# Decode attention with its MLP on one core: the place of wo's loads, the order at the last V quads, and a V quad in two pieces

## The chip, the cores and the metric

The kernel runs on one core of a Trainium2 chip. The metric is the device time of one execution in microseconds (us); of several executions the median is given. A profiled execution has a trace, from which all finer times here are taken: TensorE (PE) multiplies, and PEld is its weight load; VectorE is DVE, ScalarE is ACT, GpSimd is POOL, SyncE is SP. "SPq" is the time that an instruction which issues a DMA spends in SP's queue.

## The reference

One decode step for 8 batch rows (`B`), one token each, model width 512 (`D`). All is bfloat16 at the interfaces.

```python
x   = A_x                                        # [8, 1, 512]
q   = (layernorm(x) @ wq)                        # 32 heads of 128
k,v = k_cache[:, :, 8192-2048:, :], v_cache[...] # last 2048 positions, 8 kv heads, 4 query heads on each
p   = softmax(q k^T / sqrt(128))
h   = x + (p v as [8, 4096]) @ wo                # wo: [4096, 512], 4 MB
u   = layernorm(h)
# The second part's token shifts are zero for one token, so its first two matmuls add nothing:
x1  = u
out = h + x1 + gelu(layernorm(x1) @ w3) @ w4     # w3: [512, 1792], w4: [1792, 512]
```

The window is 2048 positions, so K and V are 4 MB for each row, 64 MB in all. With wq and wo (4 MB each) and w3 and w4 (1.8 MB each) the core reads 79.2 MB.

## The kernel before, in words

**Loads.** K and V of a row come in two quads each, (row, 0) and (row, 1), of 2 MB: four kv heads with 2048 positions. A quad is one DMA with 128 rows of 16 KB, and lands in one of the `NS` = 8 slots of the tile `ring`. The list `loads` (L240 to L247) is written out by hand; SP issues it in this order, on one hardware queue (L435 to L452): wq, then for each row b its two K quads and the two V quads of row b-2 (`LAG` = 2). After K of row 7 come V (5,0), (5,1), (6,0), (6,1), then wo in four parts of 1 MB (128 x 8 rows of 1 KB each), then V (7,0) and (7,1), and behind the list w3 and w4 (w4 in two parts). `place` numbers the quads in this order; quad n goes to slot n modulo 8 and waits for `taken` of quad n-8, the TensorE operation that read the slot last. wo shares the tile `wbig` with wq and waits only for the q projection, which is over near 17 us. w3 and w4 use the slots of K (7,0) and K (7,1). The last V quad, `LASTV`, is issued as four DMAs of 512 KB with a semaphore each (`sem_l`); `landed` says which semaphore a piece waits for.

**Compute.** Each quad has four pieces (`cq`), so that there are 64 items for K and as many for V. A written-out loop over p orders the instructions of every engine. In step p TensorE transposes item p of K (`pe_T`, 16 matmuls against a permutation, L275), ScalarE and VectorE copy the halves to SBUF (`evict`), TensorE multiplies item p-24 of V (`pe_PV`, 16 matmuls, L365; `LPV` = 24) and item p-2 of K with q (`pe_QK`, L295). The steps of a row's softmax (`softmax_1` to `softmax_5`, L304 to L355) lie between; within a step they stand ahead of `pe_PV`, and `pe_QK` behind it. K's items end at p = 63, so V of row 5 is multiplied at p = 64 to 71, row 6 at 72 to 79 and row 7 at 80 to 87. The last two `pe_QK` of row 7 stand in TensorE's queue behind the first V items of row 5. Each engine runs its own instructions in order.

**The end.** `scale` (L374, VectorE) turns the sums of a quad into `oT_all`. `pe_wo(0)` multiplies heads 0 to 15 with wo (64 matmuls, L388, after four that add x, L384), `pe_wo(1)` heads 16 to 31. In the kernel before, `scale` of quad (7,0) follows its last piece, then comes piece 0 of (7,1), then `pe_wo(0)`, then pieces 1 to 3 of (7,1), the second `scale` and `pe_wo(1)`. Behind that run the layernorm (L471 to L499), w3 (56 matmuls, L490), gelu (L515), w4 (56 matmuls, L527), the transpose and the store.

Of the kernel before, what the change touches and what calls it, by code (L numbers as in the profile page):

```python
# [14 lines left out]
DH = 128  # L15
# [11 lines left out]
NS = 8  # L27
# [6 lines left out]
LAG = 2  # L34
# [32 lines left out]
def bass_sequential_preLN__sliding_block_cached__mixer_s_mlp__decode_kernel(  # L67
# [23 lines left out]
    with es:  # L91
        sb = lambda shape, dtype, name: es.enter_context(nc.sbuf_tensor(name, shape, dtype))
        ps_t = lambda shape, dtype, name: es.enter_context(nc.psum_tensor(name, shape, dtype))
        S = lambda name: es.enter_context(nc.semaphore(name))
# [25 lines left out]
        ring = sb([128, NS, NCQ * DH], dt.bfloat16, "ring")  # L120
# [46 lines left out]
        oT_ps = ps_t([128, 512], dt.float32, "oT_ps")  # L167

        sem_r = [S(f"sem_r{i}") for i in range(NS)]
        sem_l = [S(f"sem_l{i}") for i in range(4)]  # L170
        sem_x, sem_wq, sem_wo, sem_w3, sem_w4a, sem_w4b, sem_out = (
            S(n) for n in ("sem_x", "sem_wq", "sem_wo", "sem_w3", "sem_w4a", "sem_w4b", "sem_out"))
        PE, AC, DV, PO, SP = (Engine(S(n)) for n in ("s_pe", "s_act", "s_dve", "s_pool", "s_sp"))

        def dma(eng, dst, src, sem, *waits):
            def f(e):
                e.dma_start(dst, src).then_inc(sem, 16)
            eng.op(f, *waits, inc=False)
# [62 lines left out]
        for b in range(NB + LAG):  # L241
            if b < NB:
                loads += [("k", b, 0), ("k", b, 1)]
            if b == NB + LAG - 1:
                loads += [("wo", n, 0) for n in range(4)]
            if b >= LAG:
                loads += [("v", b - LAG, 0), ("v", b - LAG, 1)]  # L247
        quads = [l for l in loads if l[0] != "wo"]
        place = {l: n for n, l in enumerate(quads)}
        LASTV = ("v", NB - 1, 1)  # L250
        taken = {}

        def landed(l, cq):
            n = place[l]
            if l == LASTV:
                return sem_l[cq], 16
            return sem_r[n % NS], 16 * (n // NS + 1)

        e_Tlo, e_Thi, e_lo, e_hi, e_QK, e_PV = {}, {}, {}, {}, {}, {}
# [2 lines left out]
        LAST = NB - 1  # L262

        def split(i):
            return i // 8, (i // 4) % 2, i % 4

        def pe_T(i):
            b, j, cq = split(i)
            s = place["k", b, j] % NS

            def half(lo):
                def f(e):
                    for c in range(lo, lo + 8):
                        n = 16 * cq + c
                        ins = e.matmul(kT_ps[i % 2][:, c * 128:(c + 1) * 128],  # L275
                                       ring[:, s, n * DH:(n + 1) * DH], ident_p[:, :], is_transpose=True)
                    return ins
                return f
            e_Tlo[i] = PE.op(half(0), landed(("k", b, j), cq), e_lo.get(i - 2), e_idp)
            e_Thi[i] = PE.op(half(8), e_hi.get(i - 2))  # L280
            taken["k", b, j] = e_Thi[i]

        def evict(i):
            e_lo[i] = AC.op(lambda e: e.activation(kT_sb[:, i % NKT, 0:1024], kT_ps[i % 2][:, 0:1024], ACT.Copy),  # L284
                            e_Tlo[i], e_QK.get(i - NKT))
            e_hi[i] = DV.op(lambda e: e.tensor_copy(kT_sb[:, i % NKT, 1024:2048], kT_ps[i % 2][:, 1024:2048]),  # L286
                            e_Thi[i], e_QK.get(i - NKT))
# [15 lines left out]
        def softmax_1(b):  # L303
            e_max[b] = DV.op(lambda e: e.tensor_reduce(mcol[:, :], S_ps[b % 2][:, :], AX.X, ALU.max),  # L304
                             e_QK[8 * b + 7], e_mT.get(b - 1))

        def softmax_2(b):
            e_mT[b] = PE.op(lambda e: e.matmul(sm[0:1, MROW], mcol[:, :], ident_f[:, :], start=True, stop=True),  # L308
                            e_max[b], e_rL.get(b - 1), e_idf)
            e = DV.op(lambda e: e.tensor_reduce(Mrow[:, :].rearrange("o (h x) -> o h x", h=4),  # L310
                                                sm[0:1, MROW].rearrange("o (h c x) -> o h x c", h=4, c=4),
                                                AX.X, ALU.max), e_mT[b])
            m_bc = bass.AP(tensor=Mrow[:, :].tensor, offset=0, ap=[[H, 1], [8, 4], [0, 4], [1, 8]])
            e_neg[b] = DV.op(lambda e: e.tensor_scalar(negrow[:, :].rearrange("o (h c x) -> o h c x", h=4, c=4), m_bc,
                                                       -1.0, None, ALU.mult), e, e_negps.get(b - 1))

        def softmax_3(b):
            e_negps[b] = PE.op(lambda e: e.matmul(sm[:, NEG], negrow[0:1, :], ones_f[0:1, 0:1],  # L318
                                                  start=True, stop=True), e_neg[b], e_ones)
            j = b % 2  # L320
            e_negc[b] = DV.op(lambda e: e.tensor_copy(negcol[:, j:j + 1], sm[:, NEG]), e_negps[b], e_exp.get(b - 2))  # L321
            e_exp[b] = AC.op(lambda e: e.activation(P_sb[:, :], S_ps[j][:, :], ACT.Exp, bias=negcol[:, j:j + 1],  # L322
                                                    scale=1.0, accum_out=lcol[:, j:j + 1]),
                             e_negc[b], e_sp.get((b - 1, 3)), e_lsel.get(b - 2))
            for r in range(4):
                a, m = P_sb[:, 128 * r:128 * (r + 1)], mask_b[:, :]
                pb = bass.AP(tensor=a.tensor, offset=a.offset, ap=[a.ap[0], [1, 128], [0, 4]])
                mb = bass.AP(tensor=m.tensor, offset=m.offset, ap=[m.ap[0], [0, 128], [1, 4]])
                eng = DV if b == LAST else PO
                e_sp[b, r] = eng.op(lambda e, r=r, pb=pb, mb=mb: e.tensor_tensor(  # L330
                    P4_sb[:, 128 * r:128 * (r + 1), :], pb, mb, ALU.mult),
                    e_exp[b], e_PT.get((b - 1, 3)), e_mask)
# [60 lines left out]
        for p in range(NG + LPV):  # L393
            if p < NG:
                pe_T(p)
                evict(p)
            for b in range(NB):
                base = 8 * b + 7 + LQK
                if p == base + 1:
                    softmax_2(b)  # L400
                elif p == base + 2:
                    softmax_3(b)
                elif base + 4 <= p <= base + 6:
                    softmax_4(b, p - base - 4)
                elif p == base + 7:
                    softmax_5(b)
            i = p - LPV
            if 0 <= i < NG:
                b, j, cq = split(i)
                if (b, j) == (LAST, 1):  # L410
                    dst = kbank[1][:, 0:16]
                    pe_PV(i, dst, e_lo[NG - 1], e_hi[NG - 1], e_lo[NG - 2], e_hi[NG - 2])
                else:
                    dst = oT_ps[:, 16 * j:16 * (j + 1)]
                    pe_PV(i, dst, e_scale.get((b - 1, 1)))
                if (b, j) == (LAST, 0) and cq == 3:
                    scale(b, 0, dst, e_PV[i])
                elif (b, j) == (LAST, 1) and cq == 0:
                    pe_wo(0)
                elif b < LAST and j == 1 and cq == 3:  # L420
                    scale(b, 0, oT_ps[:, 0:16], e_PV[i])
                    scale(b, 1, oT_ps[:, 16:32])
                elif (b, j) == (LAST, 1) and cq == 3:
                    scale(b, 1, dst, e_PV[i])
                    pe_wo(1)
            if 0 <= p - LQK < NG:
                pe_QK(p - LQK)
                b, j, cq = split(p - LQK)
                if (j, cq) == (1, 3):
                    softmax_1(b)  # L430
            if p >= 7 + LQK + 6 and (p - 7 - LQK - 6) % 8 == 0 and (p - 7 - LQK - 6) // 8 < NB:
                softmax_4((p - 7 - LQK - 6) // 8, 3)
# [3 lines left out]
        for l in loads:  # L436
            what, b, j = l
            if what == "wo":
                n, hh = b, H // 4
                dma(SP, wo_v[:, n * hh:(n + 1) * hh, :],  # L440
                    A_wo[n * hh * DH:(n + 1) * hh * DH, :].rearrange("(h p) n -> p h n", p=DH), sem_wo, e_q)
                continue
            n = place[l]
            src = (A_k_cache if what == "k" else A_v_cache)[b, 4 * j:4 * (j + 1), W0:SK, :].rearrange(
                "h (p c) d -> p h (c d)", p=32)
            free = taken[quads[n - NS]] if n >= NS else None
            if l == LASTV:
                for cq in range(4):
                    cs = slice(16 * cq * DH, 16 * (cq + 1) * DH)
                    dma(SP, ring[:, n % NS, cs], src[:, :, cs], sem_l[cq], free)  # L450
            else:
                dma(SP, ring[:, n % NS, :], src, sem_r[n % NS], free)  # L452

# [57 lines left out]
        for n in range(2):  # L511
            cs = slice(n * FH * B, (n + 1) * FH * B)
# [64 lines left out]
```

## Time and profile before

| what | value |
|---|---|
| median of 3 runs | 200.34 us (199.55, 200.34, 200.67) |
| profiled execution | 200.1 us |
| its span | 198.3 us |
| mean granted TensorE clock | 0.853 |
| HBM read | 79.18 MB, 399 GB/s over the span |
| TensorE matmul busy | 151.0 us (76%), 2861 matmuls and 2861 weight loads |
| VectorE, ScalarE, GpSimd busy | 82.5 us, 79.1 us, 32.2 us |
| K quads: 16 of 2 MB | 27.4 us from issue to landing (median) |
| V quads: 15 of 2 MB | 20.4 us |
| V pieces: 4 of 512 KB | 12.2 us |
| wo: 4 of 1 MB | 29.4 us |
| w3; w4 in two parts | 16.8 us; 19.6 and 16.5 us |

The span runs from the first to the last recorded instruction; the 1.8 us between it and the execution's time lie around it. "From issue to landing" holds the time in which a DMA stands behind others in the queue, so it is a measure of the backlog. In rows of the chain and of the timeline the first number is the start and the second the length, both in us. A line of DMA counters such as "q8 instruction: 22, 0.36, 0.6%" gives a queue's packets, MB and share of the 16 DMA engines' time. In the rows of the windows, each engine's busy time and count stand in the order PE, PEld, DVE, ACT, POOL, then the granted clock, the DMA engines' share and GB/s.

### The profile page before, as it was taken

The page shows a single profiled execution, that of the slowest core. Times are in us where ns is not written, and L with a number is a line of the kernel's source. Part 1 is how long each engine was busy: PE and PEld are TensorE (multiplying, and loading weights), DVE is VectorE, ACT ScalarE, POOL GpSimd, SP SyncE. Part 2 cuts the span into 40 slices and gives each one's busy share as a digit, 9 for nine tenths or more (in the row PEclk, how much of TensorE's full clock was granted, in tenths as well). Part 3 has the DMA queues.
Part 4 walks back from the last instruction along what each step waited for, and adds up shares of the span by engine and source line. Part 5 has one row for each costly group of instructions (what it writes and reads, how often), then busy time and mean ns, then how long its engine had stood idle before and what let it go on. Part 6 is the DMA issues. An engine that isn't in the chain of part 4 may idle for free.

```text
span 198.3 us, 6194 instructions
## 1 busy us (share of the span) xinstructions
PE 151.0 (76%) x2861; PEld 125.3 (63%) x2861; DVE 82.5 (42%) x198; ACT 79.1 (40%) x91; POOL 32.2 (16%) x38
## 2 busy tenths in 40 slices
PE   0037999889959995999199959995999865708653
PEld 0037777577747884788188848784888555708653
DVE  7401556557535444535134534443345465100041
ACT  5001676957724652465046524741365240000021
POOL 8000000340700250044001700260007000000000
PEclk9999999999987999799969996997599965555555
DMA  6999999999999999999999999999999999999960
GB/s 226 449 413 426 426 426 430 433 433 418 433 430 433 426 426 423 430 435 426 423 430 426 436 430 426 426 426 433 426 430 433 413 383 320 378 414 416 401 234 2
DMA packets 11785, 79.57 MB, mean 401 GB/s; under 512 B 744, under 2 KB 6640, under 8 KB 7664
## 3 DMA queue, kind: packets, MB, share of 16 engines
q1 hardware_dynamic: 11744, 79.18, 95.9%
q8 instruction: 22, 0.36, 0.6%
q10 hardware_dynamic: 16, 0.01, 0.1%
q14 instruction: 3, 0.02, 0.0%
HBM read 79.18 MB, written 0.01 MB: 399 GB/s over the span
## 4 chain that ended last, share of the span: by engine, by line
DMA 55%; PE 36%; DVE 4%; issue 2%; ACT 1%; SPq 0%; ACTq 0%
DMA ring<-in_A_k_cache_dram 49%; PE kT_ps L275 17%; DMA ring<-in_A_v_cache_dram 6%; PE oT_ps L365 6%; PE S_ps L295 5%; PE S_ps L388 2%; PE sm L340 2%; DVE P_sb L330 1%; PE kT_ps L365 1%; PE S_ps L527 1%; DVE pT_sb L345 1%; PE sm L353 1%; PE sm L318 1%; PE sm L308 1%; ACT L515 1%
## 5 line engine op out<-in xcount | busy, mean ns | idle before, releaser
L284 ACT ACTIVATE kT_sb<-kT_ps 128x1024 bf16<-128x1024 bf16 x64 | 65.3, 1023 | 76.1 <-PE kT_ps L275 75.5
L275 PE MATMUL kT_ps<-ident_p,ring 128*128 128x128 bf16 x1024 | 74.4, 231 | 12.8 <-DMA ring<-in_A_k_cache_dram 12.8
L275 PEld LDWEIGHTS kT_ps<-ident_p,ring 128*128 128x128 bf16 x1024 | 63.3, 104 | 28.0 <-DMA ring<-in_A_k_cache_dram 14.0
L286 DVE COPY kT_sb<-kT_ps 128x1024 bf16<-128x1024 bf16 x64 | 44.2, 691 | 68.6 <-PE kT_ps L275 68.5
L330 POOL TENSOR_TENSOR P_sb<-P_sb,mask_b 128x512 bf16<-128x512 bf16 x28 | 28.2, 1039 | 119.6 <-PE kT_ps L275 86.5
L365 PE MATMUL oT_ps<-pT_sb,ring 128*128 128x16 bf16 x960 | 32.4, 172 | 6.7 <-DMA ring<-in_A_v_cache_dram 6.7
L365 PEld LDWEIGHTS oT_ps<-pT_sb,ring 128*128 128x128 bf16 x960 | 30.8, 101 | 8.4 <-DMA ring<-in_A_v_cache_dram 6.7
L295 PE MATMUL S_ps<-kT_sb,qwin 128*32 128x512 bf16 x256 | 27.5, 414 | 0.0
L340 PE MATMUL sm<-ident_b,P_sb 128*128 128x128 bf16 x128 | 13.2, 230 | 5.7 <-DVE pT_sb L345 2.4
L345 DVE COPY pT_sb<-sm 128x512 bf16<-128x512 bf16 x32 | 13.4, 418 | 5.3 <-PE sm L340 5.3
L340 PEld LDWEIGHTS sm<-ident_b,P_sb 128*128 128x128 bf16 x128 | 8.5, 101 | 8.1 <-issue 4.5
L502 ACT ACTIVATE s<-vsum,eps 128x8 f32<-128x8 f32 x1 | 0.3, 301 | 28.8 <-DVE vsum L499 28.8
L295 PEld LDWEIGHTS S_ps<-kT_sb,qwin 128*32 128x32 bf16 x256 | 6.8, 94 | 2.9
L226 PE MATMUL S_ps<-xlnT,wbig 128*128 128x8 bf16 x128 | 3.6, 168 | 6.4 <-DMA wbig<-in_A_wq_dram 6.4
L322 ACT ACTIVATE P_sb<-S_ps,negcol 128x512 bf16<-128x512 f32 x8 | 5.5, 687 | 7.3 <-DVE negcol L321 7.3
L226 PEld LDWEIGHTS S_ps<-xlnT,wbig 128*128 128x128 bf16 x128 | 3.5, 104 | 6.5 <-issue 6.5
L374 DVE TENSOR_TENSOR oT_all<-oT_ps,rL 128x16 bf16<-128x16 f32 x15 | 2.3, 220 | 11.3 <-PE oT_ps L365 11.3
L304 DVE TENSOR_REDUCE mcol<-S_ps 128x1 f32<-128x512 f32 x8 | 5.5, 688 | 2.0 <-PE S_ps L295 1.8
L216 PE MATMUL sm<-ident_b,xln_b 8*128 8x8 bf16 x4 | 0.3, 175 | 6.5 <-DVE xln_b L198 6.5
L353 PE MATMUL sm<-lsel,ones_f 128*128 128x32 f32 x16 | 3.9, 330 | 1.3 <-DVE lsel L349 1.3
L233 DVE TENSOR_SCALAR qwin<-S_ps 128x32 bf16<-128x32 f32 x8 | 0.9, 180 | 9.3 <-PE S_ps L226 9.3
L353 PEld LDWEIGHTS sm<-lsel,ones_f 128*128 128x128 f32 x16 | 3.4, 260 | 1.8 <-DVE lsel L349 1.8
(72 smaller groups left out, 69.0 us busy)
## 6 DMA issues: line engine op xcount, KB each, us to landing
ring<-in_A_k_cache_dram SPq DMA_DIRECT2D x16, 2048.0 KB, 27.4
ring<-in_A_v_cache_dram SPq DMA_DIRECT2D x15, 2048.0 KB, 20.4
wbig<-in_A_wq_dram SPq DMA_DIRECT2D x1, 4096.0 KB, 12.3
wbig<-in_A_wo_dram SPq DMA_DIRECT2D x4, 1024.0 KB, 29.4
ring<-in_A_v_cache_dram SPq DMA_DIRECT2D x4, 512.0 KB, 12.2
ring<-in_B_w_dram SPq DMA_DIRECT2D x1, 1792.0 KB, 16.8
ring<-in_B_w_dram SPq DMA_DIRECT2D x1, 1280.0 KB, 19.6
ring<-in_B_w_dram SPq DMA_DIRECT2D x1, 512.0 KB, 16.5
```

The costliest lines, as they stand in the source:

```text
L226: ins = e.matmul(S_ps[0][:, h * B:(h + 1) * B], wq_v[:, kc, h * DH:(h + 1) * DH], xlnT[:, kc * B:(kc + 1) * B], start=(kc == 0), stop=(kc ...
L275: ins = e.matmul(kT_ps[i % 2][:, c * 128:(c + 1) * 128], ring[:, s, n * DH:(n + 1) * DH], ident_p[:, :], is_transpose=True)
L284: e_lo[i] = AC.op(lambda e: e.activation(kT_sb[:, i % NKT, 0:1024], kT_ps[i % 2][:, 0:1024], ACT.Copy), e_Tlo[i], e_QK.get(i - NKT))
L286: e_hi[i] = DV.op(lambda e: e.tensor_copy(kT_sb[:, i % NKT, 1024:2048], kT_ps[i % 2][:, 1024:2048]), e_Thi[i], e_QK.get(i - NKT))
L295: ins = e.matmul(S_ps[b % 2][32 * h:32 * (h + 1), :], qwin[:, b, 4 * j + h, w0:w0 + 32], kT_sb[:, i % NKT, :].rearrange("p (c h k) -> p h ...
L304: e_max[b] = DV.op(lambda e: e.tensor_reduce(mcol[:, :], S_ps[b % 2][:, :], AX.X, ALU.max), e_QK[8 * b + 7], e_mT.get(b - 1))
L322: e_exp[b] = AC.op(lambda e: e.activation(P_sb[:, :], S_ps[j][:, :], ACT.Exp, bias=negcol[:, j:j + 1], scale=1.0, accum_out=lcol[:, j:j + 1]),
L330: e_sp[b, r] = eng.op(lambda e, r=r, pb=pb, mb=mb: e.tensor_tensor(P4_sb[:, 128 * r:128 * (r + 1), :], pb, mb, ALU.mult), e_exp[b], e_PT.g ...
L340: ins = e.matmul(pT_ps[:, x * 128:(x + 1) * 128], P4_sb[:, 32 * c:32 * (c + 1), :].rearrange("p k h -> p (k h)"), ident_b[:, :], is_transp ...
L345: e_pT[b, r] = DV.op(lambda e: e.tensor_copy(pT_sb[:, b % NB3, 4 * r:4 * (r + 1), :].rearrange("p c n -> p (c n)"), pT_ps[:, :]), e_PT[b, ...
L353: e_Lb[b] = PE.op(lambda e: e.matmul(sm[:, LB], ones_f[:, :], lsel[:, :], start=True, stop=True), e_lsel[b], e_pT[b, 3])
L365: ins = e.matmul(dst, ring[:, s, n * DH:(n + 1) * DH], pT_sb[:, b % NB3, c, :].rearrange("p (h c j r) -> p c j h r", h=4, c=4, j=2)[:, cq, j],
```

## The change

The change has three parts, and moves no tile.

1. wo's four loads stand directly behind K of row 7 in `loads`, ahead of V of rows 5, 6 and 7. `place`, and with it every quad's slot, is as before.
2. The second-last V quad, (7,0), is issued as two DMAs (pieces 0 and 1, pieces 2 and 3) with a semaphore each; the last, (7,1), stays in four. `sem_l` has six semaphores.
3. `pe_wo(0)` stands directly behind `scale` of quad (7,0), ahead of all of quad (7,1).

```diff
-        sem_l = [S(f"sem_l{i}") for i in range(4)]
+        sem_l = [S(f"sem_l{i}") for i in range(6)]
...
-            if b == NB + LAG - 1:
+            if b == NB - 1:
                 loads += [("wo", n, 0) for n in range(4)]
...
-        LASTV = ("v", NB - 1, 1)
+        pieces = {("v", NB - 1, 0): (2, 4), ("v", NB - 1, 1): (1, 2, 3, 4)}
+        piece_sem = iter(sem_l)
+        piece_sem = {l: [next(piece_sem) for _ in ends] for l, ends in pieces.items()}
         taken = {}
 
         def landed(l, cq):
             n = place[l]
-            if l == LASTV:
-                return sem_l[cq], 16
+            if l in pieces:
+                return piece_sem[l][next(n for n, end in enumerate(pieces[l]) if cq < end)], 16
             return sem_r[n % NS], 16 * (n // NS + 1)
...
                 if (b, j) == (LAST, 0) and cq == 3:
                     scale(b, 0, dst, e_PV[i])
-                elif (b, j) == (LAST, 1) and cq == 0:
                     pe_wo(0)
...
-            if l == LASTV:
-                for cq in range(4):
-                    cs = slice(16 * cq * DH, 16 * (cq + 1) * DH)
-                    dma(SP, ring[:, n % NS, cs], src[:, :, cs], sem_l[cq], free)
+            if l in pieces:
+                for lo, hi, sem in zip((0,) + pieces[l], pieces[l], piece_sem[l]):
+                    cs = slice(16 * lo * DH, 16 * hi * DH)
+                    dma(SP, ring[:, n % NS, cs], src[:, :, cs], sem, free)
             else:
                 dma(SP, ring[:, n % NS, :], src, sem_r[n % NS], free)
```

## The prediction

> **What bounds the kernel now.** I read the page's slices and DMA queues first, then the chain of waits from 166 us on, the DMA issues one by one, and the windows between. The slices show the 16 DMA engines full until 190 us: 79.2 MB in order through one queue. So the end is the last bytes' arrival plus what the cores still do. The chain of waits (start, length, what) shows that:
>
> ```profile
> 166.20 12.70 DMA ring<-in_A_v_cache_dram
> 178.90 0.05 issue
> 178.94 1.88 PE oT_ps L365 x64
> 180.82 0.43 PE kT_ps L365 x16
> 181.25 0.24 PE S_ps L384 x4
> 181.48 1.80 PE S_ps L388 x64
> 183.28 1.46 issue
> 184.73 1.47 PE kT_ps L365 x48
> ...
> 189.81 0.51 PE kT_ps L490 x13
> 190.32 0.60 issue
> 190.92 0.22 PE kT_ps L490 x3
> ...
> 193.99 1.67 PE S_ps L527 x56
> ```
>
> V quad (7,0) lands at 178.90 (issued 166.20, 12.70 to landing) and TensorE starts at once. The pieces of (7,1), issued at 168.88, 169.53, 170.19 and 170.83, take 11.3, 11.9, 12.4 and 13.1 us: 180.2, 181.4, 182.6, 183.9. So at 183.28, when wo's first half is done, pieces 0 to 2 are there, and TensorE still stands for 1.46 us under "issue". It stands again 0.60 us at 190.32. Between the two stalls lie 48+64+2+13 = 127 matmuls, each with its weight load: some 255 instructions. The queue table gives the reason:
>
> ```profile
> q8 instruction: 22, 0.36, 0.6%
> ```
>
> 0.36 MB in 22 packets is 16.4 KB each, and TensorE's 2861 matmuls and 2861 loads make 260 instructions for each. So TensorE's program comes in blocks of about 256, and the stalls stand where one ends. The DMA rows of 182 to 183.3 us and of 188 to 189.5 us each hold one such packet, and those of 179 to 182.3 us none:
>
> ```profile
> q8 instruction: 1, 0.02, 4.3%
> ```
>
> ```profile
> q8 instruction: 1, 0.02, 3.9%
> ```
>
> I read it as two buffers: when TensorE enters a block, the one after it is asked for. 127 matmuls back from 183.28 are 64+4+16 and the last 43 of quad (7,0): the block was entered at its 21st, 178.94+21x0.0294 = 179.56. The next was usable at 184.73, 5.17 us later; the one after that 190.92-184.73 = 6.19 us later. From 179.5 on the tail runs at this pace. That is a reading of two stalls, not a direct record.
>
> The Trainium skill, Runtime: NRT & Kernel Launch, Instruction fetch mechanics, says that blocks of 16 KiB, 256 instructions, are refilled by the sequencer's own DMA queue and that a crossing is mostly hidden. The trace agrees on the block; it differs on hidden, by 1.46 and 0.60 us.
>
> The loads' issues (start, time in the queue) and the windows (length, TensorE, its loads, VectorE, ScalarE, GpSimd; granted clock, DMA share, GB/s):
>
> ```profile
> 115.80 1.25 SPq L177 DMA_DIRECT2D ring<-in_A_k_cache_dram  x2
> 127.04 9.35 SPq L177 DMA_DIRECT2D ring<-in_A_v_cache_dram  x4
> 136.44 29.71 SPq L177 DMA_DIRECT2D wbig<-in_A_wo_dram  x4
> 166.20 5.24 SPq L177 DMA_DIRECT2D ring<-in_A_v_cache_dram  x5
> ```
>
> ```profile
> 142.00:158.00 16.00, 15.06 (x295) 12.17 (x293) 8.13 (x19) 7.69 (x9) 4.04 (x4) 0.95 1.01 429
> 158.00:174.10 16.10, 10.53 (x262) 9.14 (x258) 6.56 (x18) 2.06 (x3) 0.00 (x0) 0.58 1.03 364
> 174.10:186.00 11.90, 5.60 (x195) 5.44 (x196) 0.23 (x1) 0.00 (x0) 0.00 (x0) 0.50 1.00 412
> ```
>
> K and V move at 412 to 429 GB/s, the stretch with wo at 364. The queue takes wo's 1 KB rows slowly: one issue lasts 25 us.
>
> **The change, part by part.** The sum is made against the profiled execution, 200.1 us (span 198.3 and 1.8 around it), 0.24 under the median of 200.34.
>
> *wo behind K of row 7.* The same bytes stand ahead of V (7,1), so its landings stay: cost 0, as long as wo takes what it took (V (6,1) landed at 135.79+27.6 = 163.4, wo's last part at 163.57+10.5 = 174.1: 10.7 us). Moved are four issues past V of rows 5 and 6 on SP's queue; no slot is waited for late, since rows 3, 4 and K of 6 free theirs before. A blocked issue, 25 us, now stands ahead of V (5,0), while the queue is full. GpSimd issues nothing here.
>
> V of rows 5 and 6 comes some 10.7 us later. V (5,0): 147.1 (127.04+20.1) to 157.9, against its first use at 156.91. So TensorE stands 1.0 us ahead of the last two QK groups, and row 7's softmax, queued behind, moves by 1.0: from 169.3 to 170.3. V (6,1) lands at 178.90-4.83 = 174.1; its 64 matmuls (1.88) and the scalings (0.31) end at 176.4. The cover is 172.3+1.0 against 174.1: softmax may slip 0.8 us more for nothing, and 5 us before quad (7,0)'s second half waits.
>
> *V (7,0) in two pieces.* The quad took 178.90-174.07 = 4.83 us, so the first half lands at 176.5, and 32 matmuls (0.94) run before the rest lands. Quarter pieces took 1.25 us each, 5.0 a quad, so two halves cost between 0 and 0.17; I take 0.06. The end of the quad's matmuls moves from 180.82 to 178.96+0.04+0.94 = 179.94. The added issue (0.6 us of SP) lies in front of w4's issues, which block for 4.4 and 9.3 us anyway; the added wait on TensorE is worth 0 to 0.05.
>
> *wo's first half ahead of quad (7,1).* It now waits openly for the scaling, 0.31 us by the same step at 186.20 to 186.51, which 16 matmuls covered before. 179.94+0.31+2.04 = 182.29. Then the 64 matmuls of (7,1): piece 0 until 182.76; the block's end is here. This block was entered at the 21st matmul of (7,0), now at 176.5+0.05+0.62 = 177.2, so the next is usable at 182.4 to 183.4 (lags 5.17, 6.19). Pieces 1 and 2 follow to 183.7 (184.3), the last lands at 183.99: end 184.5 (184.8) against 186.20, a gain of 1.4 to 1.7.
>
> *What is late next.* w3's matmuls would start 3.61 us after (189.81-186.20): 188.1. w3 was issued at 171.47 and took 16.8 us: 188.3, with the 0.06 188.4. Its 13 matmuls of the old block end at 188.9; the new block is usable 6.19 us after 182.8 to 183.4: 189.0 to 189.6. Before it was 190.92: a gain of 1.3 to 1.9. If a block's packet (now near 186) delays w3's slowest part by its own few tenths to 0.9 us, 1.1. From here to the end is as before; w4's last part landed at 176.51+16.5 = 193.0, needed at 193.99+40/56x1.67-1.65 = 193.5. So no gain over 2.1 is possible without earlier bytes. TensorE's granted clock stays at 0.50 in the tail. I take **1.65**: 200.1-1.65 = 198.45, on the median **198.7**.
>
> By the page's rule that the refill is hidden, the stall at 190.32 would not return and w3's landing would set 188.9: a gain of 2.0, 198.3.
>
> **The rivals.** *The block comes no earlier* (the two-buffer reading is wrong): TensorE stands until 184.73 whatever it did before, and of (7,1) 48 matmuls remain, ending 186.2 as before: no gain, 200.3. For: two stalls are little evidence; against: the packets come 6 to 10 us apart with TensorE's pace. Chance 0.13.
>
> *wo moves slower where it now stands.* At 142 to 153 us all engines are busy, and its rows of 1 KB fell to 314 GB/s in the window of 162 to 166 us even beside idle engines. 4.19 MB at 314 is 13.4 us instead of 10.7, 2.7 later for all V: 198.7+2.7 = 201.4, **slower**. It decides when wo takes more than 12.4 us. Against: K and V run at 429 beside busy engines, so SBUF traffic doesn't show. Chance 0.09.
>
> *Split loads lose the rate.* Halves that don't overlap would pay their latency twice; by w_out's short store, 1.4 us to landing, that is 1.4 later for (7,0)'s second half and all behind: 200.1, no change. Against: quarters landed 1.25 us apart. Chance 0.04. The Trainium skill, DMA: Bandwidth & Descriptors, Bandwidth, asks for batches of 1 MiB or more and gives that size 6.15 us; by it two halves would take 12.3, far off the quad's 4.83. The quarters' 1.25 us disagree.
>
> *The dips go.* In 158 to 174 us the rate was 63 GB/s under K's: 1.0 MB, 2.4 us. If the queue, no longer held by wo ahead of V, keeps its rate, V (7,1) lands up to 2.4 us earlier: about half, 197.5. Against: 1 KB rows are slow wherever they stand. Chance 0.08.
>
> **How the numbers follow.** A measurement tells about 0.5%, 1.0 us. The forecast holds 0.66, of which 0.06 ends within 1.0 us. Faster: 0.60+0.08 and 0.03 of the blocks' rival, for a block that comes only partly earlier, = 0.71; same: 0.06+0.10+0.04 = 0.20 less 0.01 for runs that scatter; slower: 0.09+0.01 = 0.10. The range 197.5 to 200.4 leaves out the slower case and some of the lowest; the likeliest case's own is 198.2 to 199.3.
>
> **What would show it.** Right: the first 32 matmuls of (7,0) start near 176.5, wo's first 64 end by 182.4, quad (7,1) ends at 184.4 to 184.9, no "issue" over 0.7 us ahead of it, and one of some tenths inside w3. Wrong: (7,1)'s last piece lands after 185, wo takes over 12 us from K (7,1)'s landing, or a stall of 1.5 us stands ahead of (7,1)'s later pieces.

## The result, and the profile after

The changed kernel takes 198.88 us in the median of 20 runs (198.28 to 199.85), the kernel before 200.33 in 20 runs beside it (199.55 to 200.67): a ratio of 0.9931, 95% interval 0.9919 to 0.9944. By the medians that is 1.45 us less; the forecast was 198.7. The profiled execution took 198.78 us with a span of 197.0, so 1.32 under that of before.

The end of the chain of waits after (start, length, what), which answers to the rows from 166 us on shown of before:

```profile
150.41 28.41 DMA ring<-in_A_v_cache_dram
...
178.86 1.03 PE oT_ps L367 x32
...
182.34 0.43 PE kT_ps L367 x16
182.78 0.70 issue
183.47 1.47 PE kT_ps L367 x48
...
188.55 0.51 PE kT_ps L491 x13
189.06 0.54 issue
189.60 0.22 PE kT_ps L491 x3
```

The last half of V (7,0) lands at 150.41+28.41 = 178.82, as the whole quad did before (178.90), so the bytes come no earlier. Only 32 matmuls are left behind it. The stall ahead of the last 48 V matmuls is 0.70 us instead of 1.46 and ends 1.26 earlier; the one inside w3 is still there, 0.54, and ends 1.32 earlier, which is the whole gain.

TensorE's timeline shows a third stall, which the chain leaves out because the landing of the second half, at 178.82, covers it (start, length, what, and in brackets the idle time before and what ended it):

```profile
172.12 3.74 PE L367 MATMUL oT_ps<-pT_sb,ring 128*128 128x16 bf16 x128
176.43 0.70 PE L367 MATMUL oT_ps<-pT_sb,ring 128*128 128x16 bf16 x20 [0.56 <-DMA ring<-in_A_v_cache_dram]
177.56 0.47 PE L367 MATMUL oT_ps<-pT_sb,ring 128*128 128x16 bf16 x12 [0.43 <-issue]
```

A block of TensorE's program ends behind the 20th matmul of (7,0). It is missing for 0.43 us here and was not before, when TensorE had stood ready since 172.3. From this place on the three block ends lie at 177.56, 183.47 and 189.60, 5.91 and 6.13 us apart: the tail goes at the pace of the blocks.

The records of the instruction queue bear this out. The three late blocks answer to one packet each, in 175 to 176.3 us, in 181 to 182.1 and in 187 to 188.3:

```profile
q8 instruction: 1, 0.02, 4.2%
q8 instruction: 1, 0.02, 5.0%
q8 instruction: 1, 0.02, 4.5%
```

None moved in 172.7 to 175, 177.56 to 181 and 183.5 to 187, the stretches that begin where TensorE enters a block. In the kernel before, TensorE stood idle from 172.30 to 178.94, and no packet moved between 173 and 182.3: the next block was fetched only after TensorE went on.

The loads and the windows after:

```profile
117.75 27.33 SPq L177 DMA_DIRECT2D wbig<-in_A_wo_dram  x4
145.13 11.99 SPq L177 DMA_DIRECT2D ring<-in_A_v_cache_dram  x10
```

```profile
142.00:158.00 16.00, 13.18 (x253) 10.63 (x249) 8.06 (x19) 7.42 (x9) 4.03 (x4) 1.00 1.06 402
158.00:174.00 16.00, 10.86 (x223) 8.62 (x223) 6.25 (x16) 2.06 (x3) 0.00 (x0) 0.50 1.00 425
```

wo blocks SP's queue as before, now from 117.75 to 145.1, and the slow stretch moves with it: 402 GB/s in 142 to 158 us where 429 stood, 425 in 158 to 174 where 364 stood. wo's last part was issued at 142.48 and took 10.7 us, so it landed at 153.2, 10.8 us behind the last K quad (117.11+25.3 = 142.4).

### The profile page after: what moved, and what is told of

It reads as the page before. It is cut to its first block, busy times and chain, and to the rows that moved or that the text cites. A ratio compares the mean times of both kernels' runs of the same rounds, so it can differ in the third digit from the quotient of the medians.

```text
span 197.0 us, 6195 instructions
## 1 busy us (share of the span) xinstructions
PE 151.6 (77%) x2861; PEld 125.7 (64%) x2861; DVE 82.5 (42%) x198; ACT 79.2 (40%) x91; POOL 32.2 (16%) x38
## 4 chain that ended last, share of the span: by engine, by line
DMA 63%; PE 32%; issue 1%; ACT 1%; DVE 1%; SPq 0%; ACTq 0%; DVEq 0%
DMA ring<-in_A_k_cache_dram 48%; PE kT_ps L277 16%; DMA ring<-in_A_v_cache_dram 14%; PE oT_ps L367 5%; PE S_ps L297 4%; PE S_ps L390 2%; PE kT_ps L367 1%; PE S_ps L528 1%; PE sm L342 1%; ACT L516 1%; PE sm L355 1%; SPq L177 0%; PE sm L310 0%; PE sm L320 0%; PE kT_ps L491 0%
## 5 line engine op out<-in xcount | busy, mean ns | idle before, releaser
L277 PEld LDWEIGHTS kT_ps<-ident_p,ring 128*128 128x128 bf16 x1024 | 63.2, 104 | 27.3 <-DMA ring<-in_A_k_cache_dram 14.0
L367 PE MATMUL oT_ps<-pT_sb,ring 128*128 128x16 bf16 x960 | 32.9, 172 | 5.1 <-DMA ring<-in_A_v_cache_dram 4.7
L297 PE MATMUL S_ps<-kT_sb,qwin 128*32 128x512 bf16 x256 | 27.3, 410 | 0.0
## 6 DMA issues: line engine op xcount, KB each, us to landing
ring<-in_A_v_cache_dram SPq DMA_DIRECT2D x4, 512.0 KB, 26.6
```

What stands on the lines that cost most here:

```text
L277: ins = e.matmul(kT_ps[i % 2][:, c * 128:(c + 1) * 128], ring[:, s, n * DH:(n + 1) * DH], ident_p[:, :], is_transpose=True)
L297: ins = e.matmul(S_ps[b % 2][32 * h:32 * (h + 1), :], qwin[:, b, 4 * j + h, w0:w0 + 32], kT_sb[:, i % NKT, :].rearrange("p (c h k) -> p h ...
L367: ins = e.matmul(dst, ring[:, s, n * DH:(n + 1) * DH], pT_sb[:, b % NB3, c, :].rearrange("p (h c j r) -> p c j h r", h=4, c=4, j=2)[:, cq, j],
```

## The experiments

The theory: the tail goes at the pace of TensorE's program blocks, of some 256 instructions; a block is asked for when TensorE enters the one ahead of it, and is usable 5 to 6 us later. The change pays because the half quad lets TensorE enter a block earlier. Rivals: the gain comes from wo's early loads, from the order at the end, or the stalls belong to other things than blocks.

**The three parts one by one, and two of them together.** The edits, against the changed kernel; the first three undo two parts each, the last undoes part 1:

```diff
 wo_early_only, wo_half_first_only:
-        pieces = {("v", NB - 1, 0): (2, 4), ("v", NB - 1, 1): (1, 2, 3, 4)}
+        pieces = {("v", NB - 1, 1): (1, 2, 3, 4)}
 wo_early_only, halves_only:
                     scale(b, 0, dst, e_PV[i])
+                elif (b, j) == (LAST, 1) and cq == 0:
                     pe_wo(0)
 halves_only, wo_half_first_only, halves_and_half_first:
-            if b == NB - 1:
+            if b == NB + LAG - 1:
                 loads += [("wo", n, 0) for n in range(4)]
```

Expected of halves_only: 

> Part 2 alone: V (7,0) in two DMAs; wo's loads and its first half where they were before. Theory (the tail goes at the pace of TensorE's program blocks, each usable 5.2 to 6.2 us after the one ahead of it is entered): the first 32 matmuls of (7,0) start near 176.5, a block is entered at the 21st, 177.1, the next is usable near 182.3 to 183.2, the one after it, inside w3, near 189.1. About 1.8 us less than before in the profile, 198.5 in the median, so faster than the whole change by 0.3. Rival (the gain comes from wo's early loads and the smoother queue): no gain, 200.3.

Expected of wo_early_only: 

> Part 1 alone: wo's loads behind K of row 7; V (7,0) in one DMA, wo's first half behind piece 0 of (7,1). Theory: the last V lands where it did, (7,0) starts at 178.9, its block is entered at 179.5 as before and the next comes near 184.7 to 185.4: 200.3 to 200.9, no gain or a small loss, with row 7's softmax some 3 us later than before. Rival: wo's early loads bring the gain, 199.

Expected of wo_half_first_only: 

> Part 3 alone: wo's first half ahead of quad (7,1); loads as before, (7,0) in one DMA. Theory: the block is entered at 179.5 as before, so TensorE stands until 184.7 whatever it did before, and wherever wo's half stands: 200.3, no gain. Rival (the order at the end carries the gain, the stall being tied to the switch from wo to V): 199.5 or less, and no stall of over 0.5 us ahead of (7,1)'s pieces.

Expected of halves_and_half_first: 

> Parts 2 and 3, wo's loads at their old place. Theory: row 7's softmax ends at 169.3 as before, V of row 6 is done at 172.3, so the stall of 0.43 us inside (7,0)'s first half goes; the block is entered at 177.1, the next at about 182.8, the one inside w3 at about 189.0: 198.4 in the median, 0.4 us under the whole change. Rival (wo's early loads bring the gain): 200.3.

| kernel | median, us | ratio to before, 95% interval |
|---|---|---|
| halves_only | 198.13 | 0.9904 (0.9891 to 0.9918) |
| wo_early_only | 200.15 | 1.0006 (0.9996 to 1.0015) |
| wo_half_first_only | 200.19 | 1.0004 (0.9995 to 1.0013) |
| halves_and_half_first | 198.06 | 0.9904 (0.9889 to 0.9920) |

All four fall on the theory's side. The half quad alone makes the gain; the other two parts alone give nothing. The two kernels with it came out 0.3 to 0.4 us under their expected times; the kernel before, at 200.10 beside them, was 0.23 lower too. The block that was expected late inside w3, at 189.0 and 189.1, isn't late: the first 16 matmuls of w3 run without a stand, until 188.91 in halves_and_half_first. With the half quad and wo's loads at their old place, TensorE's timeline (here halves_and_half_first) has no stall under "issue" left at the end, only waits for landings and for VectorE:

```profile
176.27 1.02 PE L367 MATMUL oT_ps<-pT_sb,ring 128*128 128x16 bf16 x32 [4.98 <-DMA ring<-in_A_v_cache_dram]
...
182.10 1.43 PE L367 MATMUL kT_ps<-pT_sb,ring 128*128 128x16 bf16 x48
183.85 0.60 PE L367 MATMUL kT_ps<-pT_sb,ring 128*128 128x16 bf16 x16 [0.32 <-DMA ring<-in_A_v_cache_dram]
...
188.34 0.57 PE L491 MATMUL kT_ps<-uT,ring 128*128 128x8 bf16 x16 [0.78 <-DVE hsq L480]
```

In wo_half_first_only wo's half stands ahead of all of (7,1), but starts no earlier (181.54 against 181.41), since it now waits 0.40 us for the scaling; behind piece 0 TensorE stands until the block comes, at 185.02 against 184.73 before:

```profile
183.26 0.57 PE L367 MATMUL kT_ps<-pT_sb,ring 128*128 128x16 bf16 x16
185.02 1.45 PE L367 MATMUL kT_ps<-pT_sb,ring 128*128 128x16 bf16 x48 [1.19 <-issue]
```

**The blocks themselves.** To move the block ends and nothing else, 64 matmuls with unused results were put at the head of the kernel before, where TensorE waits for wq.

```diff
+        def pe_pad(e):
+            for _ in range(64):
+                ins = e.matmul(S_ps[1][:, 0:8], ident_b[:, :], ident_b[:, 0:8], start=True, stop=True)
+            return ins
+        PE.op(pe_pad, e_idb)
         e = PE.op(pe_xT, e_xln, e_idb)
```

> The kernel before with 64 matmuls of 8 columns added at the head of TensorE's program, where it waits for wq; nothing else changes, but every block of 256 instructions ends 64 matmuls earlier in the work. Theory (the stalls stand where a block ends, and a block is usable 5.2 to 6.2 us after the one ahead of it is entered): no stall ahead of the last 48 matmuls of (7,1) and none inside w3; instead a block is entered near 181.5, at the head of wo's first half, and the next is missing inside wo's second half, behind some 16 of its matmuls, for 1.5 to 2.5 us. About 199.9, within half a us of before. Rival (the stalls belong to the switch from wo to V and to w3): 1.5 us and 0.6 us at the places of before.

```profile
183.09 1.43 PE L370 MATMUL kT_ps<-pT_sb,ring 128*128 128x16 bf16 x48
184.84 0.59 PE L393 MATMUL S_ps<-oT_all,wbig 128*128 128x8 bf16 x16 [0.32 <-DVE oT_all L379]
186.78 1.45 PE L393 MATMUL S_ps<-oT_all,wbig 128*128 128x8 bf16 x48 [1.35 <-issue]
...
189.66 0.59 PE L495 MATMUL kT_ps<-uT,ring 128*128 128x8 bf16 x16 [0.51 <-DVE uT L480]
```

The old stalls are gone, and one of 1.35 us stands behind 16 matmuls of wo's second half, as foretold; it is a little shorter than the 1.5 to 2.5 given. The rival, which ties the stalls to the switch from wo to V and to w3, is out. The time was 199.0, ratio 0.9953 (0.9934 to 0.9972), better than the 199.9 expected: here one stall of 1.35 us takes the place of two, 1.46 and 0.60, and 64 useless matmuls speed the kernel up.

**Why a block is late.** The kernel before without the loads of w3 and w4 and without the waits for them (the MLP multiplies old data, so this is a probe and no version to use; the waits are not shown here):

```diff
-        dma(SP, w3_sb, ..., sem_w3, w_free[0])
-        dma(SP, w4_sb[:, 0:FA, :], ..., sem_w4a, w_free[1])
-        dma(SP, w4_sb[:, FA:FC, :], ..., sem_w4b)
```

> The kernel before without the loads of w3 and w4 and without the waits for them: the MLP multiplies what the slots hold from K of row 7. Theory (a block comes late because its packet stands among the loads): the stall at 183.3 stays to within 1 us, since V still moves; the second block is asked for at 184.7 with the queue empty and comes within some 4 us, so the stall of 0.60 us inside w3 goes: a span 0.6 us or more shorter. Rival (a block takes 5 to 6 us whatever else is loaded): 0.60 us inside w3 stays.

```profile
184.01 1.45 PE L365 MATMUL kT_ps<-pT_sb,ring 128*128 128x16 bf16 x48 [0.77 <-issue]
...
189.09 0.59 PE L487 MATMUL kT_ps<-uT,ring 128*128 128x8 bf16 x16 [0.51 <-DVE uT L472]
```

The stall inside w3 is gone, and the first is 0.77 us instead of 1.46. The span is 196.9, 1.4 shorter, in one run. In this run the first block's way is 184.01-179.54 = 4.47 us (entered at the 21st matmul of (7,0) again, 178.92+0.62), where it was 5.17. w3's landing is not waited for here either, but in the kernel before it was not late, so the 0.60 is the block's. The second block shows the loads' part best: it is entered at 184.01, and its packet moves in 185.1 to 186.5 us:

```profile
q8 instruction: 1, 0.02, 5.7%
```

In the kernel before, that block is entered at 184.73, and its packet moves only in 188 to 189.5. So the loads lengthen a block's way; how much, one run can't say closely.

**What early loads of wo cost.**

```diff
-            if b == NB - 1:
-                loads += [("wo", n, 0) for n in range(4)]
             if b >= LAG:
                 loads += [("v", b - LAG, 0), ("v", b - LAG, 1)]
+            if b == NB - 1:
+                loads += [("wo", n, 0) for n in range(4)]
```

Expected of wo_behind_v5: 

> The whole change, but wo's loads behind V of row 5, ahead of V of row 6. Theory (what wo's early place costs is that V of row 5 comes late, with it row 7's softmax, V of row 6 and the entry into a block): V of row 5 lands as before, the softmax ends near 169, the 64 matmuls of (6,0) run as soon as that quad lands, near 169, the block is entered in time and the 0.43 us inside (7,0)'s first half goes, as does the rest: 198.1, as with wo behind V of row 6. Rival (V of row 6 late is enough, or wo must stand just ahead of V of row 7): 198.8, as the whole change.

Expected of wo_early_and_halves (part 3 undone as above): 

> Parts 1 and 2; wo's first half behind piece 0 of (7,1) as before. Theory (part 3 does nothing, because the block and the bytes set the pace): 198.8, as the whole change, with a stall of some 0.4 us inside (7,0)'s first half and one ahead of (7,1)'s later pieces. Rival (part 3 hides the stall): 199.2 or more.

With wo two quads later the time was 198.11, ratio 0.9906 (0.9886 to 0.9926). V (6,0) then lands as late as in the whole change, at 169.0 against 148.47+20.6 = 169.1, but row 7's softmax does not move:

```profile
167.80 0.63 PE L355 MATMUL sm<-lsel,ones_f 128*128 128x32 f32 x2 [0.67 <-DVE lsel L351]
169.06 1.88 PE L367 MATMUL oT_ps<-pT_sb,ring 128*128 128x16 bf16 x64 [0.62 <-DMA ring<-in_A_v_cache_dram]
```

So it is the softmax, held by V of row 5, that makes the block's entry late, and not V of row 6. wo_early_and_halves took 198.9, ratio 0.9941 (0.9922 to 0.9961), like the whole change: part 3 does nothing that can be told here. Its stalls were 0.55 us (0.4 expected), 1.30 and 0.31, against 0.43, 0.70 and 0.54 in the whole change; the time is the same within the intervals, since a block comes when it comes, whatever TensorE does meanwhile.

**The better version beside the whole change**, on one chip, and one step more:

```diff
 quarters (on halves_and_half_first):
-        sem_l = [S(f"sem_l{i}") for i in range(6)]
+        sem_l = [S(f"sem_l{i}") for i in range(8)]
...
-        pieces = {("v", NB - 1, 0): (2, 4), ("v", NB - 1, 1): (1, 2, 3, 4)}
+        pieces = {("v", NB - 1, 0): (1, 2, 3, 4), ("v", NB - 1, 1): (1, 2, 3, 4)}
```

Expected of after_again: 

> The whole change once more, beside the version with wo's loads at their old place. Theory (early wo costs some 0.7 us by the late entry into a block): 198.7 to 198.9, over that version. Rival (the two differ by the chip and the hour only): the same time.

Expected of best_again: 

> Parts 2 and 3, wo's loads at their old place, once more beside the whole change. Theory: 198.1, some 0.7 us under the whole change, with no stall of TensorE from 176.5 us to w3 but for landings. Rival: the same time as the whole change.

Expected of quarters: 

> Parts 2 and 3 with wo's loads at their old place, and V (7,0) in four DMAs instead of two. Theory (without late blocks the landings of V (7,1), w3 and w4 set the pace): the first piece's matmuls start 1.2 us earlier, near 175.2, and nothing behind (7,1) moves: 198.1. Rival (the entry into a block still sets the pace, and an earlier entry helps): 197.6 or less.

The whole change took 198.61 us (198.50 to 198.93, ratio 0.9935, 0.9918 to 0.9951), without part 1 it took 198.06 (197.97 to 198.23, ratio 0.9905, 0.9886 to 0.9924). The ranges of the runs don't touch: part 1 costs 0.55 us here, a little under the 0.7 expected, and the version without it beats both kernels. Quarters gained nothing, 198.32 (0.9916, 0.9900 to 0.9932). It is no test of an earlier entry, though: its first piece starts at 175.34, but the 21st matmul lies in the second piece, at 176.65+0.12 = 176.8, where the halves enter at 176.9. Without late blocks the bound has moved to the bytes; best_again's w3 waits for its load:

```profile
188.29 0.57 PE L491 MATMUL kT_ps<-uT,ring 128*128 128x8 bf16 x16 [0.74 <-DMA ring<-in_B_w_dram]
```

## Why the prediction was right, and where it was off

*The block reading* was right, and the forecast rests on it. It placed the two stalls that were forecast of the changed kernel, and in the experiment the one of the padded kernel. The rival in which the block comes no earlier is out. The signs named for "right" came, two of them at the edge: the stall ahead of (7,1)'s later pieces is 0.70 us where no more than 0.7 was allowed, and the quad ends at 184.94 where 184.4 to 184.9 was given. The third stall, inside (7,0)'s first half, was not foreseen.

That the sum came within 0.33 us of the profiled time (198.45 against 198.78) is in part luck: two errors of opposite sign met. Early loads of wo cost 0.55 us where the sum has nothing, and without them the refills are hidden, which the sum did not take: halves_and_half_first, the kernel that the sum in effect describes, took 197.89 and, as best_again, 198.06 in its profiled executions, 0.4 to 0.6 under it.

*The half quad*: 176.5 and 178.96 foretold, 176.4 and 178.8 landed (149.76+26.6, 150.41+28.4); the split cost nothing, so the rival in which split loads lose the rate is out. Quad (7,0) ended at 179.89 against 179.94.

*wo's first half ahead*: foretold to end at 182.29, it ended at 182.34. The end of quad (7,1) was given as 184.5 to 184.8 and came at 184.94; the block ahead of it came at 183.47, just past the 183.4 given. But the text let part 3 stand as a step of the gain, and the runs show that it carries none: with wo's half behind or ahead, the time is the same.

*wo's early loads*: the term that failed. They were costed at nothing, with a slip of 1.0 us for row 7's softmax. The softmax's last matmul came at 171.68 against 168.26: 3.4 us. In the kernel before and after:

```profile
156.91 0.55 PE L365 MATMUL oT_ps<-pT_sb,ring 128*128 128x16 bf16 x16
...
168.26 0.64 PE L353 MATMUL sm<-lsel,ones_f 128*128 128x32 f32 x2 [0.67 <-DVE lsel L349]
```

```profile
159.41 0.60 PE L367 MATMUL oT_ps<-pT_sb,ring 128*128 128x16 bf16 x16 [3.30 <-DMA ring<-in_A_v_cache_dram]
159.94 0.62 PE L297 MATMUL S_ps<-kT_sb,qwin 128*32 128x512 bf16 x4
...
171.68 0.64 PE L355 MATMUL sm<-lsel,ones_f 128*128 128x32 f32 x2 [0.66 <-DVE lsel L351]
```

The first V matmul of row 5 starts 2.50 us later, at 159.41 instead of 156.91, where 1.0 was given. V (5,0) landed at 145.13+14.2 = 159.3, not at 157.9; wo took 10.8 us, as costed, but this quad took 6.1 behind it instead of 4.83. Why it took 1.3 us longer isn't settled. The other 0.92 us lie between that matmul and the softmax's last one, 12.27 us against 11.35: in this stretch TensorE's matmuls run slower. Four QK matmuls take 0.62 us where they took 0.40 in the kernel before, and the granted clock in 158 to 162 us is 0.52 instead of 0.83. That part is not shown to be the price of the early loads: in wo_half_first_only, where wo's loads stand at the old place and TensorE doesn't stand there, the clock in 158 to 162 us is 0.53 as well.

The step that failed is the cover: "5 us before quad (7,0)'s second half waits". It counted landings only. The 3.4 us stayed inside it, and the quads did not wait; but TensorE entered the block that begins at the 21st matmul of row 6 (127 matmuls ahead of the stall) at about 172.7 instead of 169.3, the next was usable at 177.56 instead of being there, and this moved the two behind as well. The block's entry was foretold for 177.2 and the two ends behind it for 182.8 to 183.4 and 189.0 to 189.6; they came at 177.56, 183.47 and 189.60, so the gain was 1.32 instead of 1.65. Without part 1 the gain is the 2.0 that the text gave for hidden refills (198.06 against 200.10 and 200.03 in the two groups of runs).

*wo slower among busy engines*, the rival on the other side: out. wo took 10.8 us there, with 384 GB/s in 142 to 150 us. *The dips go*: out as well; the last V landed at 156.52+27.3 = 183.8 against 183.9.

## What to carry to other kernels

Where a matmul engine runs an unrolled tail of small instructions beside full DMA queues, count its instructions: short idle times under "issue" that lie one block's length apart can be late program blocks, and a few padding instructions at the program's head tell, since they move such a stall. Here the time to win lay in when the engine enters a block, not in what stands in front of the stall. A load moved ahead has a price at the first thing it pushes back, even if every landing behind it keeps its date; follow that slip to the next block's entry. Before a change with several parts is kept, run the parts alone: here one made the gain and one gave a quarter of it back.

## What the runs showed of the hardware that was not expected

A block's way, from entry to use, was between 4.5 us (no_w3_w4_loads, V's loads nearly drained, nothing behind them) and 6.3 us (wo_early_and_halves, 177.73 to 184.03), where V in 4 KB rows and w3 in 3.5 KB rows were moving; at the tail's 29 ns a matmul, TensorE uses up a block's 127 matmuls in about 3.7 us. A block was not fetched ahead while TensorE stood idle for 6.65 us in the kernel before. 64 matmuls with unused results at the head of the program made the kernel 0.5% faster. Splitting a 2 MB load of 16 KB rows in two of 8 KB rows cost no time in the queue.
